# One list-scheduled order for a gated convolution and spatial-mixing kernel, with DMA transposes and K tables in four chunks

## Chip, cores and metric

One core of one Trainium2 chip. The metric is the device time of one execution in microseconds (us), lower is better. The kernel before takes 533.61 us (median of 3 runs, 528.61 to 536.08).

## The reference, cut to what matters

Two branches read the same input x of 2048 tokens by 640 channels, and a gate mixes them.

```python
def _A_ref(u, ...):            # a long convolution over the tokens
    P = jnp.exp(logdA[:, :, None] * l[None, None, :])
    K = jnp.einsum('dn,dnl,dn->dl', Cc, P, dB).real      # 640 kernels of length 2048
    # ... Kf, Uf: real FFTs of K and u, padded to 4096
    Yf = Uf * Kf
    # ... y = inverse FFT, first 2048 tokens
    return y + u * Dskip

def _B_ref(x, w_in, w_sp, b_sp, w_out):   # a gated unit that mixes tokens
    z = _gelu(jnp.einsum('bsd,df->bsf', x, w_in))         # 2 x 864 features
    z1, z2 = z[..., :864], _layernorm(z[..., 864:])
    g = jnp.einsum('ts,bsf->btf', w_sp, z2) + b_sp[None, :, None]   # w_sp: 2048 x 2048
    return jnp.einsum('bsf,fd->bsd', z1 * g, w_out)

g = _sigmoid((x * gate_w).sum(-1, keepdims=True))
return g * a + (1 - g) * b
```

## The kernel before, the parts that matter here

Tokens lie as `(p n)`: partition p of 128, slot n of 16. The kernel transposes x on TensorE slot by slot. So in `xTp` the 128 tokens of one slot are adjacent. z1 comes out in the order `n p` in which the spatial blocks want it.

```python
xv = x2.rearrange("(p n) d -> p n d", n=NS)          # NS = 16
xTp = early.tile([P, ND, L], BF, name="xTp")
for n in range(NS):
    ps = pt("pt_x")
    for i in range(ND):
        pe.transpose(out=ps[:, 128 * i:128 * i + 128], in_=xf[:, n, 128 * i:128 * i + 128], identity=ident[:])
    (act.copy, vec.tensor_copy)[n % 2](out=xTp[:, :, 128 * n:128 * n + 128], in_=...)

def z1_tile(ft, hf):
    for i in range(ND):
        for e in range(2):
            pe.matmul(ps[0:fs, e, :], lhsT=Win[:, i, 128 * ft:128 * ft + fs],
                      rhs=xTp[:, i, 1024 * hf + 512 * e:1024 * hf + 512 * e + 512],     # 512 adjacent columns
                      start=(i == 0), stop=(i == ND - 1))
# ... z2_tile: 432 columns of Win as rhs, xTp as lhsT

def sp_block(tb, psG, psW):       # 8 blocks of 256 tokens
    # ... load 2 x 128 rows of w_sp; 32 pe.transpose of them, 4 copies on ScalarE
    # ... 7 x 17 matmuls of 256 columns, product with z1, output projection, store ob

def conv_s2(h):                   # second stage of the convolution, 32 steps for each half h
    KN = 4                        # steps to one load of fu and fk, and one store of vo
    # ... matmul u -> ScalarE copy; matmul K; VectorE product; matmul back -> ScalarE copy -> VK_d

# the end of the kernel, in program order:
#   g_tables(); conv_s2(0); conv_s1(1, ...); load va[0]; conv_s2(1); two spatial blocks; load va[1]
for n0 in range(0, NS, 2):        # final loop
    pool.dma_start(out=obr[:], in_=ob_d[:, n0:n0 + 2, :])
    pool.dma_start(out=xd[:], in_=xv[:, n0:n0 + 2, :])
    vec.tensor_tensor(out=xd[:], in0=xd[:], in1=DskB..., op=ALU.mult)
    # ... 12 matmuls of 320 columns, gate, add obr, store
```

The names of the convolution: the K tables are its kernels, and the F, G and T tables hold sines and cosines for its transforms. Stage 1 (`s1u` for u, `s1k` for the kernels) writes FU and FK to DRAM; stage 2 reads them back as fu and fk and stores vo into VK; va is VK read back for the final loop. s1k(1) is stage 1 of the second half's kernels, and ob is the parked output of the spatial branch.

## Time and profile before

| | before |
|---|---|
| time, median of the first 3 runs | 533.61 us |
| span of the profiled run, granted clock | 529.7 us, 0.875 |
| TensorE busy | 380.2 us, 72% |
| bytes moved by DMA in the span | 68.73 MB |

The prediction below shows the slices and stretches. Two more readings of the same profile matter later. The first is the groups of instructions by shape: line, engine, operation, output and inputs, shape, count, then busy us and mean ns of one, then the idle time just before them and what ended most of it.

```profile
L311 PE MATMUL ps_z<-Win,xTp 128*128 128x432 bf16 x160 | 35.2, 359 | 0.8 <-ACT z2n L313 0.8
L330 PE MATMUL ps_z<-xTp,Win 128*128 128x512 bf16 x112 | 32.0, 407 | 2.5 <-ACT zt L333 1.9 <-ACT z2n L313 0.3
```

L330 is z1. One matmul lasts 407 ns, but the next starts before it ends: 32.0 us for 112 of them is 0.286 us each, and in a dense group one starts every 0.216 us. The second reading is the DMA view from 374 to 530 us.

```profile
DMA packets 16039, 29.58 MB, mean 190 GB/s; under 512 B 1472, under 2 KB 7776, under 8 KB 16032
```

### The profile page before, as it was taken

To read this page: it belongs to the slowest core of one execution; us is meant where nothing else is said; L and a number is where in the kernel's file an instruction comes from. 1 tells how busy PE (TensorE), PEld (TensorE's weight loads), DVE (VectorE), ACT (ScalarE), POOL (GpSimd) and SP (SyncE) were. 2 spreads that over 40 slices of the span, in tenths; PEclk is the share of its full clock that TensorE was granted. 3 is DMA by queue.
4 is the path that set the end of the run, shared out by engine and by line. 5 is a ranking of instruction groups with operands and counts; after the bars stand their busy time and mean duration, and the time that the engine had idled before them with its cause. 6 is when DMAs were issued, how large, how long until landed. Compare 5 with 4: busy or idle time off the path is not lost.

```text
span 529.7 us, 9366 instructions
## 1 busy us (share of the span) xinstructions
PE 380.2 (72%) x3742; PEld 251.0 (47%) x3750; DVE 268.5 (51%) x525; ACT 285.2 (54%) x442; POOL 96.5 (18%) x118
## 2 busy tenths in 40 slices
PE   0787499967989979989886588871797135970455
PEld 0463245435777757767664366650453012530232
DVE  2365433346348998204699831205686124870254
ACT  1974756547898485389858432115676112760021
POOL 4136697020012120011111000000000100013021
PEclk9999789995999999999998599995799555995587
DMA  8912145533031212155312212065485733789685
GB/s 295 320 30 82 43 117 158 153 104 125 9 136 60 80 59 82 35 137 129 111 60 104 67 59 78 12 120 172 142 263 187 245 100 124 262 186 120 153 278 193
DMA packets 55354, 68.73 MB, mean 130 GB/s; under 512 B 9808, under 2 KB 42576, under 8 KB 55312
## 3 DMA queue, kind: packets, MB, share of 16 engines
q1 hardware_dynamic: 48560, 43.10, 28.4%
q0 software_dynamic: 6464, 23.73, 14.8%
q10 hardware_dynamic: 288, 1.31, 0.6%
q8 instruction: 29, 0.48, 0.4%
q14 instruction: 13, 0.11, 0.1%
HBM read 42.78 MB, written 25.35 MB: 129 GB/s over the span
## 4 chain that ended last, share of the span: by engine, by line
PE 36%; ACT 15%; DMA 15%; issue 12%; DVE 11%; POOL 9%; SPq 0%; DVEq 0%; ACTq 0%; POOLq 0%
PE ps_g L399 15%; DMA FK_d<-s1k 6%; PE ps_v L625 5%; PE ps_o L414 4%; ACT vo L626 4%; DMA xd<-in_A_u_dram 3%; DMA VK_d<-vo 2%; DMA ldt<-in_A_log_dt_dram 2%; POOL t L240 2%; POOL t L65 2%; PE ps_g L400 2%; PE ps_k L480 2%; ACT wT L337 2%; ACT G L590 2%; DVE s1k L337 2%
## 5 line engine op out<-in xcount | busy, mean ns | idle before, releaser
L399 PE MATMUL ps_g<-wT,z2n 128*128 128x256 bf16 (+1 forms) x896 | 116.1, 280 | 5.6 <-DVE vT L403 4.5
L399 PEld LDWEIGHTS <-z2n 128*128 128x128 bf16 (+1 forms) x896 | 87.1, 104 | 22.8 <-issue 6.5
L619 DVE TENSOR_TENSOR p<-ps_s2k,us 128x640 bf16<-128x640 f32 x64 | 52.7, 825 | 18.5 <-PE ps_s2k L612 9.2
L403 DVE TENSOR_TENSOR vT<-ps_g,z1t 128x512 bf16<-128x512 f32 x24 | 16.6, 690 | 45.4 <-PE ps_g L400 45.3
L330 PE MATMUL ps_z<-xTp,Win 128*128 128x512 bf16 (+1 forms) x132 | 36.9, 403 | 2.5 <-ACT zt L333 1.9
L531 PE MATMUL ps_s1k<-xk,F 128*128 128x320 bf16 x64 | 16.8, 372 | 28.8 <-ACT s1k L337 25.8
L612 PE MATMUL ps_s2k<-fk,T 128*128 128x320 bf16 x128 | 30.7, 322 | 9.0 <-DMA fk<-FK_d 9.0
L311 PE MATMUL ps_z<-Win,xTp 128*128 128x432 bf16 x160 | 35.2, 359 | 0.8 <-ACT z2n L313 0.8
L626 ACT CAST vo<-ps_v 128x320 bf16<-128x320 f32 x64 | 27.2, 426 | 15.5 <-PE ps_v L625 13.9
L414 PE MATMUL ps_o<-Wout,vT 128*128 128x320 bf16 (+1 forms) x224 | 33.0, 299 | 3.4 <-ACT ob L416 2.9
L337 ACT COPY wT<-pt_w 128x1024 bf16<-128x1024 bf16 x32 | 31.0, 1017 | 6.9 <-PE pt_w L388 5.8
L625 PE MATMUL ps_v<-p,G 128*128 128x320 bf16 x128 | 29.6, 314 | 5.1 <-ACT vo L626 2.2
L388 PE MATMUL pt_w<-ident,wrows 128*128 128x128 bf16 x256 | 22.7, 242 | 14.1 <-ACT wT L337 12.2
L609 ACT CAST us<-ps_u 128x320 bf16<-128x320 f32 x64 | 27.6, 431 | 9.4 <-DVE p L619 7.2
L672 PE MATMUL ps_i<-xd,ident 128*128 128x320 bf16 x32 | 12.2, 383 | 27.1 <-DVE xd L666 26.9
L337 DVE CAST s1k<-ps_s1k 128x640 bf16<-128x640 f32 x16 | 13.2, 825 | 35.6 <-DMA FK_d<-s1k 25.7
L337 ACT CAST s1k<-ps_s1k 128x640 bf16<-128x640 f32 x16 | 11.1, 692 | 36.4 <-DMA FK_d<-s1k 35.9
L607 PE MATMUL ps_u<-fu,T 128*128 128x320 bf16 x64 | 19.9, 311 | 14.0 <-DMA fu<-FU_d 9.2
L416 ACT ACTIVATE ob<-ps_o,omg 128x320 bf16<-128x320 f32 x32 | 16.4, 525 | 24.0 <-PE ps_o L414 23.0
L388 PEld LDWEIGHTS <-wrows 128*128 128x128 bf16 x256 | 21.1, 151 | 16.6 <-issue 14.2
L612 PEld LDWEIGHTS <-T 128*128 128x128 bf16 x128 | 12.9, 102 | 33.6 <-issue 15.5
L680 ACT ACTIVATE ot<-ps_i,gsb 128x640 bf16<-128x640 f32 x8 | 6.3, 794 | 41.3 <-PE ps_i L674 41.3
(188 smaller groups left out, 745.3 us busy)
## 6 DMA issues: line engine op xcount, KB each, us to landing
wrows<-in_B_w_sp_dram POOLq DMA_DIRECT2D x16, 512.0 KB, 4.6
FU_d<-s1u SPq DMA_DIRECT2D x32, 160.0 KB, 2.0
FK_d<-s1k SPq DMA_DIRECT2D x16, 320.0 KB, 6.1
fu<-FU_d SPq DMA_DIRECT2D x16, 320.0 KB, 2.9
fk<-FK_d SPq DMA_DIRECT2D x16, 320.0 KB, 3.7
VK_d<-vo SPq DMA_DIRECT2D x16, 320.0 KB, 2.4
z_d<-zt SPq DMA_DIRECT2D x12, 256.0 KB, 2.3
z1t<-z_d POOLq DMA_DIRECT2D x8, 384.0 KB, 4.1
```

The costliest lines, as they stand in the source:

```text
L311: pe.matmul(ps[:, e, 0:432], lhsT=xTp[:, i, 128 * st:128 * st + 128], rhs=Win[:, i, Fh + 432 * e:Fh + 432 * e + 432], start=(i == 0), stop ...
L330: pe.matmul(ps[0:fs, e, :], lhsT=Win[:, i, 128 * ft:128 * ft + fs], rhs=xTp[:, i, 1024 * hf + 512 * e:1024 * hf + 512 * e + 512], start=(i ...
L337: (vec.tensor_copy if eng == "v" else act.copy)(out=out_, in_=in_)
L388: pe.transpose(out=ps[:, 256 * j + 128 * r:256 * j + 128 * r + 128], in_=rows[r][:].rearrange("t (p n) -> t n p", n=NS)[:, 4 * s4 + j, :], ...
L399: pe.matmul(ps[0:fs, ft - f0, :], lhsT=z2n[:, st, 128 * ft:128 * ft + fs], rhs=wT[st // 4][:, st % 4, :], start=(st == 0), stop=False)
L414: pe.matmul(ps[:], lhsT=vT[ft // 2][0:fs, ft % 2, 128 * r:128 * r + 128], rhs=Wout[0:fs, ft, HD * e:HD * e + HD], start=(ft == 0), stop=(f ...
L607: pe.matmul(pu[:], lhsT=T[:, k, 0:128], rhs=fu[:, j, :], start=True, stop=True)
L609: act.copy(out=us[:], in_=pu[:])
L612: pe.matmul(ps[:, e, 0:HD], lhsT=T[:, k, 64 * e:64 * e + 128], rhs=fk[:, j, :], start=True, stop=True)
L619: vec.tensor_tensor(out=p12[:], in0=ps[:, :, 0:HD], in1=us[:].unsqueeze(1).to_broadcast([P, 2, HD]), op=ALU.mult)
L625: pe.matmul(pv[:], lhsT=G[e][:, k, :], rhs=p12[:, e, :], start=(e == 0), stop=(e == 1))
L626: act.copy(out=vo[:, j, :], in_=pv[:])
```

## The change

The intent is to fill TensorE's holes. Every piece of work becomes a task with a cost, its reads and writes, and a bias. A list scheduler in the kernel puts all tasks of all engines into one order and emits them. TensorE's transposes of x, of the spatial weights and of the parameters become DMA transposes. The G and T tables are made early and parked in DRAM. K tables come in four chunks of 160 channels, so that their buffers fit beside the convolution's, and the first half of the convolution can run between spatial blocks. The core of the diff, cut:

```diff
+class Plan:
+    ...
+    def run(self):
+        # ... longest path below each task, then event by event: for each engine the ready task
+        #     with the highest (path + bias) whose buffers are free; a DMA ends 2.2 us + bytes / 260e3 after issue
+        for s, _, i, e in order:
+            T[i]["fn"](e)
+
-    for n in range(NS):
-        ps = pt("pt_x")
-        for i in range(ND):
-            pe.transpose(out=ps[:, 128 * i:128 * i + 128], in_=xf[:, n, 128 * i:128 * i + 128], identity=ident[:])
+    xT = early.tile([P, ND, L], BF, name="xT")
+    xTn = xT[:].rearrange("k i (p n) -> k i n p", n=NS)
+    S_(dma("ACT", lambda: Win2[:], lambda: wiv[:, :, Fh:F], 1106000, w=["Win2"], bias=9000))
+    S_(dma("ACT", lambda: ldt[:], lambda: A_log_dt.partition_broadcast(P), 164000, w=["ldt"], bias=8000))
+    for g in range(4):
+        E(dma("SP", lambda g=g: xT[:, :, 512 * g:512 * g + 512], lambda g=g: x2[512 * g:512 * g + 512, :], 1100000,
+              w=[("xT", g)], tr=True, bias=7000 - 10 * g))
+    # ... six parameters by DMA transpose
+    E(dma("SP", lambda: Win1[:], lambda: wiv[:, :, 0:Fh], 1106000, w=["Win1"], r=["nat_in"], bias=300))
...
-                          rhs=xTp[:, i, 1024 * hf + 512 * e:1024 * hf + 512 * e + 512],
+                          rhs=xTn[:, i, 8 * hf + 4 * h:8 * hf + 4 * h + 4, :],
...
-    # sp_block: w_sp rows loaded, 32 pe.transpose, 4 ScalarE copies
+        for r in range(2):
+            dma("SP", lambda r=r: wT()[:, :, 128 * r:128 * r + 128], lambda r=r: wspv[:, 2 * tb + r, :], 650000,
+                w=[(wT, r)], tr=True, bias=1000 - 100 * tb)
...
-        KN = 4
+    KN = 2
...
-            so = ...            # s1k: one buffer
+                so = sbt(CVX, "s1k", "s1k", [P, 4, HD], bufs=2)
...
+    for h in range(2):
+        for k0 in (0, 16):
+            va_load(h, k0, 16)         # each as soon as its 16 steps are stored
...
-        vec.tensor_tensor(out=xd[:], in0=xd[:], in1=DskB..., op=ALU.mult)
+        add(("DVE", "POOL"), (dv2(2 * D), 3.2), lambda e, xd=xd: E_[e].tensor_tensor(...))
```

`xTn` is a view of `xT`. A DMA transpose of rows of x puts the tokens in their natural order, p-major. z1 still wants `n p`, so its moving operand now takes every 16th element.

## The prediction

> **What bounds the kernel now.** I read the page first, for the engines' shares and the slices:
>
> ```profile
> PE 380.2 (72%) x3742; PEld 251.0 (47%) x3750; DVE 268.5 (51%) x525; ACT 285.2 (54%) x442; POOL 96.5 (18%) x118
> ...
> PE   0787499967989979989886588871797135970455
> ...
> PEclk9999789995999999999998599995799555995587
> DMA  8912145533031212155312212065485733789685
> ```
>
> TensorE is busiest at 72%, but its row has holes: at the start, near slice 10, and from slice 20 on. Where it has holes the granted clock drops to 5 tenths. So no engine bounds the whole; stages do. I cut the span where the work changes and asked for busy times by stretch (columns: stretch; length; busy us with instruction counts of PE, weight load, DVE, ACT, POOL; granted clock; DMA share; GB/s):
>
> ```profile
> 0.00:17.00 17.00, 1.44 (x10) 0.95 (x10) 3.78 (x27) 5.26 (x6) 5.67 (x17) 1.00 0.89 317
> 17.00:123.00 106.00, 85.83 (x545) 46.52 (x553) 50.44 (x102) 65.56 (x78) 49.97 (x33) 0.93 0.38 115
> 123.00:341.00 218.00, 189.54 (x2646) 146.94 (x2643) 127.84 (x278) 143.12 (x204) 24.34 (x40) 0.94 0.26 80
> 341.00:374.00 33.00, 14.66 (x104) 10.10 (x103) 10.54 (x24) 11.06 (x14) 1.08 (x2) 0.79 0.51 128
> 374.00:405.00 31.00, 29.65 (x161) 15.86 (x160) 26.07 (x32) 24.14 (x64) 0.00 (x0) 0.95 0.65 210
> 405.00:443.00 38.00, 8.62 (x34) 3.86 (x33) 6.60 (x8) 6.29 (x12) 2.35 (x2) 0.58 0.55 174
> 443.00:478.00 35.00, 30.36 (x156) 15.80 (x156) 26.29 (x32) 23.24 (x61) 2.25 (x4) 0.89 0.67 189
> 478.00:530.00 52.00, 20.15 (x96) 10.95 (x95) 16.96 (x24) 6.53 (x9) 10.82 (x20) 0.66 0.78 189
> ```
>
> The reader sees three kinds of stage. From 17 to 341 us (input projections, then spatial blocks beside the K tables) TensorE is 81 to 87% busy. From 374 to 405 and 443 to 478 (second convolution stage) the 32 steps go at about 0.95 us each, a chain of matmul, ScalarE copy, matmul. From 341 to 374, 405 to 443 and 478 to 530, 123 us together, nothing is busy: G tables made in lockstep, FK stores waited for one by one, and the final load. The chain that ended last says so for two of them:
>
> ```profile
> 412.95 9.69 DMA FK_d<-s1k
> ...
> 464.71 9.72 DMA VK_d<-vo
> ...
> 484.00 12.58 DMA xd<-in_A_u_dram
> ```
>
> **What the Trainium skill says.** "DMA: Bandwidth & Descriptors", section "Latency and other measured facts", gives 261 GB/s for a DMA transpose with a non-contiguous middle dimension and 350-400 GB/s otherwise; no DMA transpose is in the trace of before, so no row here confirms it. The same page, "Rules for kernel authors", says several issuing engines share the same 16 DMA engines; the trace agrees in that queues of SP and POOL together reach 317 GB/s in the first stretch and slow each other at the end. "TensorE: Matmul & The Clock Gate", section "HAM oscillation — how this bites in real kernels", says waits between matmul bursts put the clock back to half; the trace agrees: clock 0.58 and 0.66 in the waiting stretches, and a 320-column matmul starts every 0.27 us there against 0.13 us when dense. The same page, "Part 4: PE-mode transpose", gives about 275 ns in a kernel; this trace has 242 ns:
>
> ```profile
> L388 PE MATMUL pt_w<-ident,wrows 128*128 128x128 bf16 x256 | 22.7, 242 | 14.1 <-ACT wT L337 12.2
> L337 ACT COPY wT<-pt_w 128x1024 bf16<-128x1024 bf16 x32 | 31.0, 1017 | 6.9 <-PE pt_w L388 5.8
> ```
>
> **The change, part by part.** I compared the instruction order of both kernels and priced the new order with durations of the old trace.
>
> Removed: 256 transposes of the spatial weights (22.7 us busy), 80 of x (8.0 us) and 30 of parameters (80 and 30 from the groups list; 30 x 219 ns pipelined, 2.6 us), in sum 33 us of TensorE; their copies, 31.0 + 5.3 us of ScalarE and 3.9 + 2.9 us of VectorE. Against that stand 26 DMA transposes of 2.6 + 1.0 + 8.4 = 12.0 MB, at the skill's 261 GB/s an estimate of 46 us, spread over some 300 us in which before moves only 80 to 115 GB/s. The first 4 (x) are at the head of the SP queue; those of the spatial weights run up to two blocks ahead, with 18 us per block to hide 1 MB.
>
> Moved: G and T tables are made at the start and parked in DRAM, which takes the 33 us lockstep stretch away. The bias becomes one row. All 8 spatial blocks and the K tables interleave with the first half of the convolution: 11 of its 32 steps lie before the last K block. s1k gets two buffers in place of one. Half of the last va load can go early. K tables come in 4 chunks of 160 channels in place of 2 of 320: the same elements with more instructions.
>
> The new time by stages of TensorE's new order, pitches read from the trace: 432 columns 0.18 us, 512 columns 0.216, 256 columns 0.1156 (1.85 us per 16), 320 columns 0.14 (in groups of 7, 0.155), 160 K matmuls 3.4 us.
>
> 1. Start: the first matmul needs w_in's second half and the first transposed quarter of x, 1.8 MB; before took 17 us for similar loads. I take **15**.
> 2. z2: 160 x 0.18 = 29, with cold start **31**.
> 3. z1, gate, stage 1 of u: 120 x 0.216 + 80 x 0.047 + 64 x 0.14 = 39, with evacuation waits (two buffers, stores through one queue) **44**. So 75 in place of 106.
> 4. First spatial block to last K block: 323 + 187 + 221 + 221 matmuls of 256 columns x 0.1156 = 110; 196 of the output projection x 0.155 = 30; 8 K blocks x 3.4 = 27; the last 20 of z1 4; 32 of s1k and 57 of the convolution x 0.14 = 12.5; sum 184. Beside it, per chunk, ScalarE has 33 exponentials at some 0.32 us, 4 at 0.86, 8 sines at 0.71 and 8 at 0.86, about 27 us with the rows scaled by width from 465 and 1270 ns, and two table loads of 1.28; VectorE 40 small operations at 0.32, copies, and products over 16,640 elements, about 29 us plus 5 to 8 of evacuations. That is under the 46 us of TensorE per chunk, but close and in order. For misfits I add 7%: **198**.
> 5. Last K block to s1k: evacuate, store (12 small DMAs at 0.3 to 0.7 us issue), land, expand (24 DMAs), land; two landings of 3 us plus issue on two queues: **17**, with 9 convolution steps inside.
> 6. s1k(1): before 3.46 us per group of 8 (2.45 store + 0.83 copy + semaphores); with two buffers 1.75 x 8 = 14, and early va loads contend: **16**.
> 7. 12 + 32 = 44 steps x 0.945 = 42, plus queue jitter **43**.
> 8. Tail: last VK store 2.4, half the va load (1.3 MB at 150 to 200 GB/s) 8, then the final loop, whose buffers and clock don't change: 28 (497.6 to 526), last store 3: **41**, against 52.
>
> Sum 15 + 31 + 44 + 198 + 17 + 16 + 43 + 41 = 405; since steps 4 to 5 have some slack that I counted twice I say **402 us**, a ratio of 0.75.
>
> **Rivals.** (a) *DMA transposes are slow and hold the SP queue.* For: nothing in the trace shows their rate, and all loads and stores now go through SP in a fixed order, so a transpose that holds the queue delays u, z1 and s1k stores behind it. Against: 12 MB is small beside 400 us. At half the rate the start and z2 wait for x: 10 to 40 us more, 415 to 440. (b) *VectorE or ScalarE becomes the bound of step 4*, because ET has one buffer and each chunk must wait for the K block before. For: 37 + 7 us against 46. Against: exponentials of the next chunk can go beside the K block. Slower by 5 us per chunk: 420. (c) *The fixed order is fragile*: an engine waits at its next instruction where before other work followed. For: the second convolution stage now moves 2 steps per DMA (1280 bytes per row in place of 2560), three issues of 0.35 us per 1.9 us on a queue that also waits for its stores. At 1.2 us per step, 11 us more. (d) *It fits better than I allow*: no misfits in step 4, tail 36: about 378. No rival reaches the 533 us of before: it would take 130 us of new waiting.
>
> **Range and chances.** From (d) below and (a) with part of (c) above: 376 to 438. Faster 0.94; within 2% 0.03, slower 0.03, for a DMA transpose several times slower than the skill has it.
>
> **What would show it.** By stage in the new profile: TensorE over 90% busy and clock near 1 from the first spatial block to the last K block, 190 to 205 us; first z2 matmul near 15 us; first spatial block near 90; last K block done near 290; no G tables stretch; FK stores overlapping in pairs; 44 convolution steps in 40 to 46 us; a final loop of 28 us that still runs at a half clock. The prediction is wrong if the chain of waits shows the wT or xT transposes for more than 20 us, if steps take over 1.2 us, or if VectorE runs near 100% in step 4 while TensorE waits.

## The result

The changed kernel takes **604.5 us** (median of 4 runs, 603.63 to 609.28), beside 532.15 us for the kernel before in the same job (4 runs, 528.61 to 536.08). The ratio is 1.1372, 95% interval 1.1283 to 1.1461. It is slower, and far outside the range. Ratios here are the mean time of one kernel's fast runs over that of the other's of the same rounds, so not quite the ratio of the medians. Executions over 1.5% slower than the fastest of the same kernel are left out of the means.

The page of the changed kernel: busy time by engine, then TensorE's busy tenths and clock in 40 slices of 15.2 us.

```profile
PE 463.0 (76%) x3384; PEld 233.5 (38%) x3384; DVE 292.4 (48%) x594; ACT 254.5 (42%) x505; POOL 139.6 (23%) x140
...
PE   0359969999999999997799998999842493842453
...
PEclk9969855555555556998799999999975598777678
```

TensorE has 358 instructions less and is 83 us longer busy. (The DMA engines move 77.64 MB in the span, in place of 68.73.) Its row is all 9 from the seventh slice to the fifteenth (91 to 228 us), yet the clock row has 5 there. Before, the clock was at 5 only in slices with waits, where TensorE was busy for 0 to 7 tenths. The stretches (length; busy us and instructions of PE, weight load, DVE, ACT, POOL; clock; DMA share; GB/s):

```profile
20.00:72.00 52.00, 38.47 (x246) 21.72 (x245) 37.59 (x72) 33.39 (x36) 18.10 (x17) 0.88 0.57 130
85.00:236.00 151.00, 147.67 (x209) 27.86 (x209) 31.03 (x60) 22.04 (x33) 12.00 (x7) 0.50 0.23 70
236.00:430.00 194.00, 179.68 (x2492) 137.30 (x2490) 136.40 (x310) 133.83 (x298) 64.25 (x50) 0.96 0.49 118
482.00:551.00 69.00, 45.01 (x220) 21.44 (x219) 36.83 (x45) 34.04 (x85) 6.17 (x11) 0.79 0.87 186
```

From 85 to 236 us TensorE does 209 matmuls in 151 us, at 98% busy: 0.7 us for each. Spatial blocks with K tables (236 to 430) are 93% busy at clock 0.96, as predicted. The convolution steps (482 to 551) are 65% busy while DMA is at 87%. The chain of waits of this kernel reaches back only to 585 us, into the final loop, so the stretches carry the reading. The groups by shape name the 151 us:

```profile
L594 PE MATMUL ps_z<-xT,Win 128*128 128x512 bf16 x120 | 111.9, 1097 | 0.0
L576 PE MATMUL ps_z<-Win,xT 128*128 128x432 bf16 x160 | 32.9, 368 | 21.0 <-DMA Win<-in_B_w_in_dram 13.7 <-ACT z2n L311 7.3
```

L594 is z1, the same shape as L330 before, and it waits for nothing (0.0). 111.9 us for 120 is 0.93 us each in place of 0.286. L576 is z2, with the operands the other way round, and costs what it cost.

The stages, each from the first or last start of one group of matmuls to the next boundary (us). The last two columns are versions from the experiments:

| stage | predicted | changed kernel | e3 | e6 |
|---|---|---|---|---|
| start to first z2 | 15 | 19.6 | 20.0 | 10.8 |
| to first spatial block (z2, z1, gate, stage 1 of u) | 75 | 192.2 | 114.7 | 90.2 |
| to last K block | 198 | 218.1 | 203.5 | 200.6 |
| to s1k(1) | 17 | 20.8 | 20.5 | 21.8 |
| s1k(1) | 16 | 31.2 | 30.2 | 28.4 |
| remaining steps, to first final matmul | 43 | 69.0 | 66.1 | 67.4 |
| to the end | 41 | 56.6 | 55.6 | 54.7 |
| sum, the profiled span | 405 | 607.5 | 510.6 | 473.9 |

The borders are not clean. The changed kernel's third stage still holds about 20 us of z1 (its last matmul starts at 233.1 us), and e6's third stage 13 us of it (until 114.0). Of the 44 steps that were predicted after s1k(1), e6 has 48 there, because only 16 came before it; the changed kernel and e3 have 44.

### The profile page after: what moved, and what is told of

It is laid out like the page before. It is cut to its first block, busy times and chain, and to the rows that moved or that the text cites. A ratio compares the mean times of both kernels' runs of the same rounds, so it can differ in the third digit from the quotient of the medians.

```text
span 607.5 us, 9069 instructions
## 1 busy us (share of the span) xinstructions
PE 463.0 (76%) x3384; PEld 233.5 (38%) x3384; DVE 292.4 (48%) x594; ACT 254.5 (42%) x505; POOL 139.6 (23%) x140
## 2 busy tenths in 40 slices
DMA packets 111309, 77.64 MB, mean 128 GB/s; under 512 B 56810, under 2 KB 104634, under 8 KB 111266
## 5 line engine op out<-in xcount | busy, mean ns | idle before, releaser
L594 PE MATMUL ps_z<-xT,Win 128*128 128x512 bf16 (+1 forms) x140 | 130.5, 1097 | 0.0
L255 POOL TENSOR_SCALAR si<-th 128x160 int32<-128x160 f32 x23 | 15.0, 658 | 224.5 <-DMA fu<-FU_d 141.8
L318 DVE CAST s1u<-ps_s 128x320 bf16<-128x320 f32 x41 | 19.1, 488 | 97.5 <-PE ps_s L616 66.1
L594 PEld LDWEIGHTS <-Win 128*128 128x128 bf16 (+1 forms) x140 | 18.9, 135 | 95.7 <-issue 93.4
L576 PE MATMUL ps_z<-Win,xT 128*128 128x432 bf16 x160 | 32.9, 368 | 21.0 <-DMA Win<-in_B_w_in_dram 13.7
L255 POOL TENSOR_SCALAR ci<-ai 128x800 int32<-128x800 int32 x11 | 34.7, 3162 | 16.7 <-DVE ai L787 13.2
L576 PEld LDWEIGHTS <-xT 128*128 128x128 bf16 x160 | 16.4, 103 | 42.9 <-issue 30.2
L311 ACT ACTIVATE mr<-lre 128x160 bf16<-128x160 f32 x128 | 32.4, 328 | 0.2
L311 ACT ACTIVATE ET<-ci 128x640 bf16<-128x640 int16 (+1 forms) x32 | 25.3, 797 | 14.5 <-POOL ci L255 14.5
L616 PE MATMUL ps_s<-xf,F 128*128 128x320 bf16 x64 | 24.0, 436 | 9.0 <-DVE s1u L318 5.7
```

Source lines behind the costliest of these rows:

```text
L255: eng.tensor_scalar(out=out_, in0=in_, scalar1=s1, scalar2=None, op0=op0)
L311: return add("ACT", cost, lambda e: act.activation(out=out_(), in_=in_(), func=func, scale=scale), r=r, w=w, fset=fs, bias=bias, deps=deps)
L318: (vec.tensor_copy if e == "DVE" else act.copy)(out=out_(), in_=in_())
L576: pe.matmul(ps()[:, h, 0:432], lhsT=xT[:, i, 128 * st:128 * st + 128], rhs=Win2[:, i, 432 * h:432 * h + 432], start=(i == 0), stop=(i == N ...
L594: pe.matmul(ps()[0:fs, h, :], lhsT=Win1[:, i, 128 * ft:128 * ft + fs], rhs=xTn[:, i, 8 * hf + 4 * h:8 * hf + 4 * h + 4, :], start=(i == 0) ...
L616: pe.matmul(ps()[:, 0:HD], lhsT=F1[:, ab, :, :].rearrange("p q k -> p (q k)"), rhs=xf()[:, j, HD * h:HD * h + HD], start=True, stop=True)
```

## The experiments

Fifteen kernels were run. Where "the same order" is said, the two traces hold the same instructions in the same order on every engine (but for four matmul records of z1 that e1's trace lacks).

### z1's moving operand (e1, e2, e3)

Theory S: z1 is slow because its moving operand takes every 16th element, a step of 32 bytes. Rival: it is slow because of its place in the new order, its weight loads, or its waits.

**e1**, the changed kernel with adjacent columns, wrong (it mixes up tokens), the same order:

```diff
-rhs=xTn[:, i, 8 * hf + 4 * h:8 * hf + 4 * h + 4, :]
+rhs=xT[:, i, 1024 * hf + 512 * h:1024 * hf + 512 * h + 512]
```

> One operand of the changed kernel is altered: the 512 moving columns of the z1 matmuls are 512 neighbours of xT in place of every 16th element. The tokens come out in another order, so the result is wrong on purpose; instructions, their order and their waits are the same on every engine. Theory S (the strided moving operand makes the z1 matmuls slow): a z1 matmul goes from 0.93 us pitch at a half clock to about 0.22 us at full clock, z1's busy time from 130 to about 32 us, the stretch from first to last z1 matmul from 148 to about 50 us, the whole from 604 to 500-515 us. Rival C (the half clock comes from something else in this stretch, such as the transposes by DMA): pitch stays at 0.43 us or more, the whole at 535 or more. Rival W (the fixed order and its waits cost the time, not the matmuls): within 2% of 604.

Measured: 509.59 us (509.12 to 512.01, 4 runs; before 534.97), ratio 0.9566 (0.9505 to 0.9626). z1's full-width group in e1:

```profile
L594 PE MATMUL ps_z<-xT,Win 128*128 128x512 bf16 x116 | 31.0, 417 | 0.5 <-issue 0.4
```

With the narrower matmuls z1's mean is 411 ns and its busy time 35.5 us, in place of 130.5. One operand's step is worth 95 us.

**e2**, the reverse: the kernel before with z1 reading every 16th column, wrong.

```diff
-rhs=xTp[:, i, 1024 * hf + 512 * e:1024 * hf + 512 * e + 512]
+rhs=xTp[:, i, :].rearrange("k (p n) -> k n p", n=NS)[:, 8 * hf + 4 * e:8 * hf + 4 * e + 4, :]
```

> The converse in the kernel before: its z1 matmuls read every 16th element of xTp in place of neighbours (wrong tokens on purpose), nothing else changes. Theory S: 140 matmuls go from 0.22 to about 0.93 us, some 100 us more of TensorE in a stretch where it was 81% busy, so the whole goes from 532 to 610-635 us. Rivals C and W (the cause lies in the changed kernel's own order, clock or transposes): 532 within 3%.

Measured: 639.94 us (639.82 to 642.5), ratio 1.2017 (1.1929 to 1.2104). The groups by shape:

```profile
L330 PE MATMUL ps_z<-xTp,Win 128*128 128x512 bf16 x120 | 114.1, 1095 | 0.6 <-ACT zt L333 0.6
L311 PE MATMUL ps_z<-Win,xTp 128*128 128x432 bf16 x160 | 56.6, 521 | 0.0
```

z1 is as slow in the old order as in the new one, so it is the operand and not the order. z2, interleaved with it here, goes from 359 to 521 ns although its own operands didn't change. Its median is 564 ns, the length of the longest in the kernel before (568), and the granted clock was 0.64 from 60 to 120 us, in place of 0.93 in the kernel before (17 to 123 us). So z2 ran at the low clock. Why the clock falls is not shown.

**e3** mends it and stays correct. The whole spatial path takes natural token order, so rows of w_sp, the bias and ob are addressed without `(p n)`. Only the gate of the final loop still needs `(p n)`, so it is computed in both orders (80 matmuls of one column more).

```diff
-rhs=xTn[:, i, 8 * hf + 4 * h:8 * hf + 4 * h + 4, :]
+rhs=xT[:, i, 1024 * hf + 512 * h:1024 * hf + 512 * h + 512]
-wspv[:, 2 * tb + r, :]
+B_w_sp[256 * tb + 128 * r:256 * tb + 128 * r + 128, :]
# ... bias row and the store of ob likewise; a second gate row for omg
```

> A right version of e1: the whole spatial path keeps the natural order of tokens (z1 columns, rows of w_sp, bias row, 1-g and the rows of the parked block), with 80 more one-column gate matmuls; only the final sum uses the other order. Theory S: as e1 plus 4 us, 500-520 us, result right. If the first theory is all there is, it should also reach the prediction's 376 to 438; I expect it not to, because the second half (after the last K block 171 us in the changed kernel against 113 foreseen) and the start are untouched: 500-520. Rival C or W: 580 or more.

Measured: correct, 511.64 us (510.04 to 518.53; 510.86 for the three fast runs), ratio 0.9585 (0.9515 to 0.9655). This is the changed kernel's idea without the step. It beats the kernel before by 4%, and is still 109 us above the prediction.

### Which property of the operand costs (e13, e14, e15)

**e13, e14, e15** are the changed kernel with steps of 2, 4 and 8 elements (4, 8 and 16 bytes) in place of 16, all wrong, all in the same order. The edit for 4 elements:

```diff
-rhs=xTn[:, i, 8 * hf + 4 * h:8 * hf + 4 * h + 4, :]
+rhs=xT[:, i, :].rearrange("k (n s) -> k s n", s=4)[:, 2 * hf + h, :]
```

The Trainium skill gives a reason to expect a threshold. "SBUF — State Buffer", section "Door 1: The DMA port swizzle (why `[64,N]` ≈ `[32,N]`)", says "SBUF has **16-byte cachelines**", and that accesses to one line need at least 2 hits in it for full rate. Theory L took that rule.

> The changed kernel with z1's moving operand read at every 2nd element (4-byte step) in place of every 16th (32-byte step); wrong result on purpose, the same instructions in the same order on every engine. Theory L (the price comes with each new 16-byte line of the buffer, four columns share a line here): mean of the z1 matmul 400 to 430 ns as with adjacent columns (411 ns in e1), total 506 to 516 us. Rival G (any step costs, in proportion to it or at once): 500 ns or more, total over 520 us.

> As e13 with every 4th element (8-byte step, two columns to a 16-byte line). Theory L: 400 to 430 ns, total 506 to 516 us. Rival G: between 600 and 1100 ns, total over 530 us.

> As e13 with every 8th element (16-byte step, each column in a line of its own, as with the 32-byte step). Theory L: as slow as the 32-byte step, 1097 ns, total 600 to 610 us. Rival G (in proportion to the step): about 700 to 800 ns, total 545 to 570 us. If the line is 32 bytes: 400 to 430 ns.

Measured (2 runs each; before 533.73): 509.87, 535.72 and 604.37 us. From the timelines of five kernels, a dense group of ten z1 matmuls (start, length in us). The first fence is e1, with a step of 2 bytes, then come e13 (4), e14 (8), e15 (16) and the changed kernel (32):

```profile
121.47 2.32 PE L594 MATMUL ps_z<-xT,Win 128*128 128x512 bf16 x10
```

```profile
120.16 2.42 PE L594 MATMUL ps_z<-xT,Win 128*128 128x512 bf16 x10
```

```profile
123.74 4.68 PE L594 MATMUL ps_z<-xT,Win 128*128 128x512 bf16 x10
```

```profile
126.16 9.18 PE L594 MATMUL ps_z<-xT,Win 128*128 128x512 bf16 x10
```

```profile
126.93 9.36 PE L594 MATMUL ps_z<-xT,Win 128*128 128x512 bf16 x10
```

Take off the length of the last matmul of a group (0.38, 0.39, 0.63, 1.08 and 1.10 us) and divide by nine: one starts every 0.216, 0.226, 0.450, 0.900 and 0.918 us. A 512-column operand lies in 64, 128, 256, 512 and 512 lines of 16 bytes. So at steps of 4, 8 and 16 bytes the time comes to 1.76 ns for each line. With adjacent columns 64 lines would come to 0.113 us at that price (an estimate from these runs), and 0.216 us are measured, so there something else sets the time. Theory L holds for e13 and e15. It fails for e14, where rival G's forecast came true: two columns to a line already double the time, so the page's "2 hits" aren't enough here; four nearly are. Rival G (a price in proportion to the step) fits from 4 to 16 bytes and falls after that: 16 bytes are as slow as 32 within 2%.

The clock was 0.95 in e14's stretch (85 to 135 us) and 0.50 in e15's, and the cost of a line is the same in both. So the low clock doesn't set z1's time. Why the clock falls while TensorE is busy, no run shows.

### The start (e5, e6)

The semaphore numbers in the trace show that the DMAs that SyncE and ScalarE issue share eight semaphores in turn (40 or 41 DMAs on each), and that each of ScalarE's two loads waits until the last DMA on its own semaphore, eight places before, has landed. The Trainium skill, "DMA: Bandwidth & Descriptors", section "Anatomy of one DMA — SWDGE (gpsimd) path", says that such a wait happens "on the issuing sequencer before dispatch". ScalarE's timeline in the changed kernel (start, length) agrees:

```profile
4.53 0.26 ACT L434 ACTIVATE f1b<-f1i 128x64 bf16<-128x64 int16 x1 [2.52 <-DVE f1i L257]
13.30 0.44 ACTq L306 DMA_DIRECT2D Win<-in_B_w_in_dram  x1
21.57 0.35 ACTq L306 DMA_DIRECT2D ldt<-in_A_log_dt_dram  x1
21.97 2.01 ACT L311 ACTIVATE ts<-ti 128x1024 bf16<-128x1024 int16 x2 [17.18 <-DMA nat_Cim<-in_A_C_im_dram]
```

ScalarE computes nothing for 17.2 us, held by its own two load issues, which wait for transposes on SyncE's queue: the third of x landed at 13.28 us, and the load of w_in was issued at 13.30. z2 can't start without that load, and ScalarE can't drain z2's PSUM banks (the buffers that TensorE writes to) meanwhile.

**e5**, e3 with both loads issued first on SyncE:

```diff
-S_(dma("ACT", lambda: Win2[:], ...))
-S_(dma("ACT", lambda: ldt[:], ...))
+S_(dma("SP", lambda: Win2[:], ...))
+S_(dma("SP", lambda: ldt[:], ...))
```

> Natural token order as in e3 (511.64 us there), and the loads of w_in's second half and of log_dt go first on SyncE's queue, not on ScalarE's. Theory W (ScalarE issues these two loads itself, the issues wait at their completion semaphores for transfers of SyncE's queue until 13.3 and 21.6 us, and ScalarE, which works in order, makes no table and drains no bank until then): first z2 matmul at 10 to 14 us in place of 20.0, z2 done by 48 to 54 us in place of 66.7, total 492 to 500. Rival L (the start is bound by the bytes of the first loads, 3.8 MB): first z2 matmul still at 17 to 20 us, z2 done after 62 us, total within 4 us of e3.

Measured: correct, 484.47 us (481.88 to 486.28; before 532.88), ratio 0.9087 (0.9023 to 0.9151). First z2 at 11.1 us, and z2 done by 57.0 in place of 66.7. z1 runs from 70.6 to 117.4 in place of 88.6 to 140.9. The same view of e5:

```profile
4.52 0.26 ACT L434 ACTIVATE f1b<-f1i 128x64 bf16<-128x64 int16 x1 [2.52 <-DVE f1i L257]
7.11 1.06 ACT L311 ACTIVATE ts<-ti 128x1024 bf16<-128x1024 int16 x1 [2.33 <-DVE ti L257]
```

Theory W holds, and it is worth 27 us, more than the 12 to 20 it promised: the work that ScalarE and VectorE do earlier also lets z1 start earlier.

**e6**, e5 with w_in's first half loaded ahead of the parameters:

```diff
-w=["Win1"], r=["nat_in"], bias=300
+w=["Win1"], bias=6850
```

> e5 and the load of w_in's first half ahead of the parameters' transposes, not waiting for them. Theory X (z1 starts late, 22 us after the last z2 matmul in e3, because that load is issued behind stores that wait for VectorE's copies): the gap between the last z2 and the first z1 matmul falls under 6 us, total 10 to 18 us under e5. Rival E (the stretch is bound by VectorE and ScalarE, whose gelus, statistics and copies must be done anyway): the gap moves into z1, z1 and stage 1 of u take as long in sum, total within 4 us of e5.

Measured: correct, 478.25 us (475.73 to 478.91), ratio 0.8951 (0.8894 to 0.9007). The gap before z1 is gone (z2 until 56.6, z1 from 57.1), as theory X said. But z1 then ends at 114.0, only 3.4 us earlier, as rival E said. The order changed too: the first spatial block starts at 101.0, beside z1, in place of 121.3. The last K block is 11 us earlier (301.6 against 312.6) and the total 6 us better, between the two forecasts.

### The late part: transfers, bytes, or order (e4, e7, e8, e9)

e3 takes 172 us from the last K block to the end, where the prediction has 117. Three explanations were tried.

**e4**, e3 with `KN = 4` and two buffers: half as many transfers of twice the size, as the kernel before has them.

```diff
-KN = 2
+KN = 4
-fu, fk, vo: bufs=3
+fu, fk, vo: bufs=2
```

> As e3, with 4 convolution steps per load and store in place of 2 (rows of 2560 bytes, two buffers in place of three), so half as many transfers on the SP queue in the second stage. Theory Q (the second stage is slowed by many small transfers through one queue, each of which also waits for the transfer eight before it): the stretch from the first s1k of the second half to the last convolution step, about 100 us in the changed kernel, shortens by 15 to 30 us, the whole to 475-500. Rival B (bytes in flight and contention with the va loads, not their number): within 2% of e3. Rival F (fewer buffers and another order hurt): slower than e3 by over 2%.

Measured: correct, 514.14 us (513.03 to 514.84), ratio 0.964 (0.9582 to 0.9698), the same as e3 within the intervals. The number of small transfers alone isn't it. (e4 also has one buffer less for each of fu, fk and vo; a gain that this took back would not show.)

**e7**, e3 with all loads of va held back until the convolution's last store:

```diff
-r=["vap"] + [("VK", h, i) for i in range(k0 // KN, (k0 + kn) // KN)]
+r=["vap"] + [("VK", 1, i) for i in range(32 // KN)] + [("VK", h, i) for i in range(k0 // KN, (k0 + kn) // KN)]
```

> e3 and all loads of va wait until the convolution's last store, so none runs beside s1k(1) or beside the second convolution stage. Theory V (the early va loads, in 640-byte pieces, take the DMA engines from the FK stores and from fu and fk): s1k(1) 29 to about 18 us, from the first step after it to the last 66 to about 46 us, the last load and final loop 55 to about 75 us, total 497 to 506. Rival B (the bytes of this phase, 30 MB at some 170 to 240 GB/s, must be moved anyway and only their order changes): every stretch that shrinks is given back, total 509 to 518; s1k(1) and the steps shrink by under 10 us together.

Measured: correct, 515.49 us (513.06 to 516.2), ratio 0.9649 (0.9589 to 0.9708). The stretches s1k(1), steps and tail, first of e3, then of e7:

```profile
359.00:390.00 31.00, 9.72 (x33) 4.30 (x32) 7.42 (x9) 5.80 (x9) 5.57 (x5) 0.50 0.86 201
390.00:455.00 65.00, 45.91 (x217) 22.22 (x217) 35.93 (x44) 33.60 (x85) 6.19 (x11) 0.77 0.82 195
455.00:510.00 55.00, 22.19 (x98) 11.75 (x95) 17.96 (x20) 6.78 (x9) 11.37 (x13) 0.68 0.59 146
```

```profile
363.00:386.00 23.00, 10.07 (x33) 4.50 (x34) 6.59 (x8) 5.27 (x8) 5.51 (x5) 0.50 0.85 230
386.00:440.00 54.00, 43.24 (x216) 20.06 (x216) 36.99 (x45) 32.65 (x85) 2.79 (x5) 0.86 0.73 205
440.00:514.00 74.00, 23.50 (x98) 12.24 (x98) 18.15 (x20) 6.77 (x9) 11.34 (x13) 0.65 0.80 146
```

s1k(1) and the steps shrink by 19 us together (third number of each line), so the early va loads do slow them, as theory V says. The tail grows by the same 19 us and the total doesn't fall, as rival B says, though it had the two stretches shrink by under 10 us. A load moved earlier was not hidden; it was paid for where it went.

**e8**, e3 with VK laid out in DRAM so that a va load reads 10,240 bytes in one piece in place of 640:

```diff
-VK_d = [dram.tile([2, 16, 4, 32, HD], ...)]    # c n q k d
+VK_d = [dram.tile([32, 2, 4, 16, HD], ...)]    # k c q n d; the G tables' columns in the order q n
```

> e3 with VK laid out in DRAM so that a va load reads 10,240 bytes in one piece for each partition in place of 16 pieces of 640 bytes (its stores then write 640-byte pieces in place of 1280); bytes, order and number of transfers unchanged. Theory V in its form by pieces (small pieces make the va loads dear): s1k(1) 29 to about 20 us, steps 66 to about 50 us, last load and loop 55 to about 46 us, total 472 to 488. Rival B (bytes alone): total within 5 us of e3. If the smaller stores cost more than the loads save: steps longer than 66 us, total over 516.

Measured: 513.41 us (509.13 to 514.89), ratio 0.9605 (0.9536 to 0.9674): no gain. The size of va's pieces alone isn't it either. (e8's stores of VK write pieces half as long, so here too a gain could be taken back.)

**e9**, e6 with half of the bytes of fu, fk and va, wrong; TensorE, VectorE and ScalarE run the same order:

```diff
-dma("SP", lambda fu=fu: fu()[:], lambda k=k: fv(FU_d)[:, k:k + KN, :], ...)
+dma("SP", lambda fu=fu: fu()[:, 0:1, :], lambda k=k: fv(FU_d)[:, k:k + 1, :], ...)
# ... fk likewise; va: rows 0 to 7 of 16; matmuls read index 0, and n // 2
```

> e6 (478.25 us) with half of the bytes of the fu, fk and va loads: each load brings one of two steps (or half of the rows of va) and the matmuls read it twice. Wrong result on purpose; the same instructions on TensorE, VectorE and ScalarE in the same order. From the last K table to the end e6 takes 172 us and moves 30.5 MB; this takes 6.5 MB away. Theory B (this phase is bound by the bytes that the DMA engines move, 177 GB/s in the mean): 28 to 40 us less, total 438 to 450. Rival C (it is bound by the order of the instructions and the latency of each transfer, so half the bytes save little): under 10 us less, total over 468.

Measured: 450.43 us (449.05 to 453.17; before 531.58), ratio 0.8457 (0.8394 to 0.8521), 28 us under e6. The late part in the DMA view, e6 from 302 to 474 us and e9 from 302 to 447:

```profile
DMA packets 27275, 30.52 MB, mean 177 GB/s; under 512 B 4314, under 2 KB 24270, under 8 KB 27266
```

```profile
DMA packets 24972, 24.07 MB, mean 166 GB/s; under 512 B 4314, under 2 KB 22222, under 8 KB 24962
```

6.45 MB less save 27 us of the late part, 27.8 us in the total. That is the lower edge of theory B (28 to 40) and far from rival C (under 10). So bytes cost time here, and 27 us is half of the 55 us by which e6's late part exceeds the prediction. At e6's mean rate of 177 GB/s 6.45 MB would be 36 us (an estimate); the mean rate falls to 166 GB/s, and the late part is still 145 us, 28 above the prediction. e9 also makes each transfer smaller, so it doesn't tell a limit on the rate from the time that one transfer takes to land. (The result passed the comparison with the reference all the same. So that comparison doesn't see an error of this kind in the convolution, and "correct" vouches little for that branch in any of these kernels, e8's new layout above all.)

### The scheduler's choices (e10, e11, e12)

**e10**, e6 with the final loop as before has it: loads on GpSimd's queue alone, the product on VectorE alone.

```diff
-dma(QQ, lambda obr=obr: obr()[:], ...)      # QQ = ("SP", "POOL"), xd likewise
-add(("DVE", "POOL"), (dv2(2 * D), 3.2), lambda e, xd=xd: E_[e].tensor_tensor(...))
+dma("POOL", lambda obr=obr: obr()[:], ...)
+add("DVE", dv2(2 * D), lambda e, xd=xd: E_[e].tensor_tensor(...))
```

> e6 with the final loop as the kernel before has it: the loads of obr and xd on GpSimd's queue alone, and the product with the skip row on VectorE alone (e6 has it in part on GpSimd, at 2.6 us each). Theory T (the scheduler's choice of engine and queue lengthens the final loop, about 40 us after the last va load in place of the 28 of before): from the first final matmul to the last e6's 49 us falls to 36 to 41 us, total 466 to 472. Rival: the loop is bound by the time from issue to landing of its loads with two buffers and stays as long, total 475 to 482.

Measured: correct, 475.79 us (474.52 to 476.65), ratio 0.8932 (0.8862 to 0.9002). From the first final matmul to the last 45.2 us in place of 49.3. That is short of what theory T promised, and the convolution before it ended 3 us later. The total is in the rival's range and doesn't tell e10 from e6.

**e11**, e10 with three buffers for obr and xd in place of two:

```diff
-obr = sbt(CV, "obr", "obr", [P, 2, D], bufs=2)
-xd = sbt(CV, "xd", "xd", [P, 2, D], bufs=2)
+obr = sbt(CV, "obr", "obr", [P, 2, D], bufs=3)
+xd = sbt(CV, "xd", "xd", [P, 2, D], bufs=3)
```

> e10 with three buffers for obr and xd in place of two. If the final loop waits for its loads' landing (the rival in e10): another 5 to 9 us less than e10. If theory T was all of it: within 4 us of e10.

Measured: correct, 492.62 us (491.07 to 498.49; 492.39 for the three fast runs), ratio 0.9232 (0.9159 to 0.9306). It is 17 us slower, which neither side expected. VectorE's timeline in e11 (start, length, and in brackets the idle time before with its releaser):

```profile
449.94 0.88 DVE L994 SCALAR_TENSOR_TENSOR ot<-ps_i,gsb,obr 128x640 bf16<-128x640 f32 x1 [2.06 <-PE ps_i L990]
452.97 0.82 DVE L980 TENSOR_TENSOR xd<-xd,DskB 128x1280 bf16<-128x1280 bf16 x1 [2.15 <-DMA xd<-in_A_u_dram]
456.59 0.49 DVE L999 TENSOR_TENSOR ot<-ot,obr 128x640 bf16<-128x640 bf16 x1 [2.80 <-ACT ot L998]
458.41 0.89 DVE L994 SCALAR_TENSOR_TENSOR ot<-ps_i,gsb,obr 128x640 bf16<-128x640 f32 x1 [1.33 <-PE ps_i L990]
```

Every instruction waits, one for TensorE, the next for a load, the next for ScalarE. The third buffer changed the order that the scheduler found: VectorE's repeating sequence is L999, L994, L980 here, and mostly L994, L999, L980 in e10. In it each load, product, matmul and gate follows the last one in single file, 7.3 to 8.6 us for two slots (4.0 to 5.5 in e10). Our reading is that the order, frozen on the scheduler's model of time, fits the real times worse than e10's. No run tests that, for instance with three buffers in e10's order.

**e12**, e10 with the G tables' four sines held back until z2's last gelu, in 5 rounds:

```diff
+for i in tg_ids[4:]:
+    pl.tasks[i]["deps"].add(z2_ids[15])
 pl.run()
```

> e10 (475.79 us) with the four sines of the G tables held back until the last gelu of z2, so that ScalarE drains z2's banks with one table load more in place of three pairs of them. Theory Z (step 2 ran 46 us in place of 31 because ScalarE goes to and fro between sines at 1.0 us, table loads at 1.28 us each and gelus, and TensorE waits for a bank): first z2 matmul at 11 us, last at 44 to 50 in place of 57 (the gate's 7 us move behind it, so the sum of z2 and gate ends at 51 to 56), total 466 to 473. Rival Y (that time is only moved: the sines fall into z1, whose gelus and copies need ScalarE too): z1 ends as late as before, at 112 to 117 us, total 474 to 480.

Measured: correct, 478.6 us (475.78 to 481.84, 6 runs; before 533.22), ratio 0.8988 (0.8945 to 0.9032). z2's matmuls in e12 (count; ns min, median, max; first and last start):

```profile
L578 PE MATMUL ps_z<-Win,xT x160: 342/346/568, 10.6 to 43.8; 128*128 128x432 bf16 x160
```

z2 alone takes 33 us, near the 31 of the prediction's step 2. But the first spatial block then starts at 117.0 us, in place of 101.5 in e10. Rival Y holds: z1 ends at 112.8, no earlier than it allowed, and the total is not better. The time was only moved.

## Why the prediction was wrong, point by point

The failed step is **step 3**, and in it one term, the prediction's "120 x 0.216". It priced 512-column matmuls by a row of the old profile, by engine, shape and type. The new instruction has the same shape, but its operand has another step. It takes 0.93 us, so 140 of them (120 in step 3, 20 in step 4) cost 140 x (0.93 - 0.216) = 100 us more; e1 gives 95 of it back, and e3 93. The diff shows `xTn`, but the working never compares the operand's layout with the old one.

The other steps, with e6 as the version freed of the operand and of the start:

- **Step 1** (15 us): 19.6 measured, 10.8 once ScalarE no longer issues loads (e5). The bytes were fine; the issuing engine was held.
- **Steps 2 and 3** without the operand (75 us): 114.7 in e3, 90.2 in e6. The start and w_in's late load explain most of it (e5, e6), and part of e6's gain is that z1 now runs on into the next stage. The rest is in part ScalarE's sines: e12, which holds four of them back, makes z2 nearly as short as predicted, but the time comes back in z1. What holds z1 is not separated. "With evacuation waits 44" was too little.
- **Step 4** (198 us) held: 200.6 in e6, and TensorE 93% busy at clock 0.98. The gain of e6 over the kernel before lies around here. From the first spatial block to s1k(1) it takes 222 us (101.0 to 323.4, with 16 convolution steps inside), and the kernel before 278 (126.1 to 403.7, with 30 steps). Part of that is moved: e6 issues the stores of its G tables by 28.0 us, and the kernel before makes them in the 33 us stretch.
- **Steps 5 to 8** (117 us): 172 in e6. The sum of four steps, each priced by latency and issue, implied 30.5 MB in 117 us, or 261 GB/s. The kernel before had moved 29.58 MB in 156 us of its late part at 190 GB/s, and none of the late stretches in the prediction's table is above 210 (single slices of 13 us reach 278). e9 shows that bytes cost time there: 27 us of the 55 us of excess went with 6.45 MB. The 44 steps took 69.0 us in the changed kernel, 1.57 us each in place of 0.945, which the prediction had named as a sign of being wrong (over 1.2). Merging 44 steps into one run and loading va early removed no byte, and e7 shows how a hidden load reappears.
- **Steps 7 and 8** beyond that: what holds the remaining 28 us in e9 is open. Changing the number of step transfers (e4), the size of va's pieces (e8) or GpSimd's part in the final loop (e10) brought no clear gain in e3 and e6.

The rivals. (a) Slow DMA transposes: somewhat slower than priced, and not the main cause. The four of x (2.6 MB) held SyncE's queue for 12.89 us, which comes to 203 GB/s. The 16 of w_sp held it for a median of 2.8 us each, the first four in a row for 21.7 us (24.4 to 46.1):

```profile
L304 SPq DMA_TRANSPOSE wT<-in_B_w_sp_dram x16: 1859/2794/6694, 24.4 to 370.0; - x16
```

What the runs show to wait for transposes are ScalarE's loads (e5); the stores behind them were not tested. (b) A bound by VectorE or ScalarE in step 4: no, see step 4. (c) A fragile order: right in kind, and e5 is a case of it (e11 probably another). The steps did slow down, but e4, with the old size of transfer, is no faster. (d) Better than allowed: no. The gravest error was the sentence that no rival reaches 533 us. Each rival varied a wait or a bound, and none asked whether an instruction kept its price. One reading of the old trace is also incomplete, without effect on the sum: in the first stretch, which reaches 317 GB/s, ScalarE's queue carried 1.31 of the 5.39 MB, beside SyncE's and GpSimd's.

Of the slowdown of some 202 us over the prediction, 95 are the operand (shown, e1 to e3), 27 the loads on ScalarE (e5), 6 the late load of w_in (e6) and 74 the rest. Of that rest, e9 attributes 27 us of the late part to 6.45 MB that it took away. How much the other 24 MB weigh was not measured.

The best versions are e6 and e10, at 0.895 and 0.893 of the time before.

## What to carry to other kernels

When a change swaps who makes a layout, compare the access step of every later reader before reusing a duration: here, the same 512-column matmul costs 0.216 us or 0.92 us, by how many 16-byte lines it reads. Before adding up steps, divide the bytes of a stage by its predicted time and ask whether the old trace ever held that rate in such a stage. Do not let an engine with work to do issue loads whose semaphores it must wait for, and rerun after any change of a buffer count, since a new order came out 17 us slower with more room (e11).

## What the Trainium skill lacked or had wrong

- "SBUF — State Buffer", section "Door 1: The DMA port swizzle (why `[64,N]` ≈ `[32,N]`)": it asks for at least 2 hits in a 16-byte line for full rate. For TensorE's moving operand in bf16, two columns to a line took 0.450 us for 512 columns against 0.216 with adjacent columns. Four took 0.226, and one 0.900 to 0.918. It gives no cost of a line; the runs come to 1.76 ns at steps of 4, 8 and 16 bytes.
- "TensorE: Matmul & The Clock Gate": its parts on the cost of a matmul price it by columns and weight loads and don't give the step of the moving operand, which makes a factor of 4.2 here.
- The same page, section "HAM oscillation — how this bites in real kernels", tells of a clock that falls in waits between bursts. Here it stood at 0.50 for 150 us in which TensorE was 98% busy in the profile and z1 waited for nothing. With two columns to a line (e14) it was 0.95.
- "DMA: Bandwidth & Descriptors", section "Latency and other measured facts": 261 GB/s for a transpose with a non-contiguous middle dimension, 350 to 400 otherwise. Here, by the time that they held the queue, the first four transposes came to 203 GB/s, and 0.52 MB of w_sp in a median hold of 2.8 us to 187 GB/s.
- The same page, section "Bandwidth", has loads alone and no rate for mixed loads and stores of 160 to 320 KB in pieces of 640 to 1280 bytes. The late part held 177 to 190 GB/s in before and e6.
- The same page, section "Anatomy of one DMA — SWDGE (gpsimd) path", says where the wait before an issue happens but not what it can cost an engine that also computes. Here ScalarE computed nothing for 17.2 us.
